# Two projections moved from the front into the attention, and the maxima taken 76 scores ahead instead of 80

## The chip, the cores and the metric

The kernel runs on one core of one Trainium2 chip. The metric is the device time of one execution in microseconds, the median of the runs shown. A profiled execution gives the engines' instructions: PE is TensorE (PEld its weight loads), DVE is VectorE, ACT is ScalarE, POOL is GpSimd, SP is SyncE, whose queue issues nearly all DMAs here. An engine takes its instructions in the order in which the program emits them, and so does each queue.

## The reference

One transformer block with adaptive norms, in float32, over 2048 rows of 512 columns:

```
mod = silu(c) @ w_mod                      # six vectors: sa, ca, ga, sb, cb, gb
h = layernorm(x) * (1 + ca) + sa
q, k, v = split(h @ wqkv)                  # 32 heads of 16 columns
o = softmax(q k^T / 4) v                   # full attention, 2048 x 2048 a head
x = x + ga * (o @ wo)
h = layernorm(x) * (1 + cb) + sb
x = x + gb * (gelu(h @ w1 + b1) @ w2 + b2) # 1792 hidden columns
```

## The kernel before, in words

The rows are cut into four blocks of 512 (NB, TB) and the 32 heads into eight groups of four. One block of queries against one group of heads is a unit, 32 in all (NU), in the order block 0 groups 0 to 7, block 1, and so on. Precision comes from splitting an operand into a high and a low part (tiles of two planes, "parts"); a projection of 128 output columns of one block of rows is then a group of twelve matmuls (terms3: four high-high, four low-high, four high-low).

**The front** is an order written out by hand (SCRIPT, lines 45 to 60). It norms and transposes the four blocks of rows, computes the modulation vectors, does the first projections (token G with kind, column group and block: G110 is the keys of column group 1 for block 0) and starts the maxima of the first unit's scores: token X emits two score matmuls (L390), token x one reduction on VectorE (L395). The front ends when LEAD score matmuls have been emitted.

**The attention** is 512 half-steps (half_step). The array is used as two halves of 64 rows. A half-step emits four score matmuls for the exponentials (L647, tile e, then exp on ScalarE, L654), four score matmuls for the maxima of a later unit (L390, tile mx, then a reduction on VectorE, L395), six matmuls of a background group if there is one (L276 through bg_mm), and last the value matmuls of the step before (pv, L681). A group of twelve full matmuls is 24 half matmuls, four half-steps. The maxima run LEAD scores ahead of what the half-steps alone would give: `nx = min(64 * NU, LEAD + 4 * (hs + 1))`. They use the PSUM banks 3, 4, 5 in turn (ring "mx"), the exponentials 0, 1, 2 (ring "e"), the background bank 7 (ring "bg").

When all 64 maxima of a unit are reduced, max_rows (lines 405 to 429) makes them into two rows beside the queries: a reduction (L407) and a 32x32 transposition (L409) on VectorE, then a copy and a subtraction on GpSimd (L411, L412) that split them in a high and a low part, then an SP store to memory (L416, three clock ticks later) and an SP load into the query tile (L422, six ticks later). The exponentials of the unit read these rows. A clock tick is one exponential; a half-step has four. Small waits are written as `later(n, f)`, n ticks.

Background work comes from a generator (work, lines 998 to 1014): block0 yields the projections left over from the front (the list plan), then comes front(b) (output projection, residual, layer norm and transposes of query block b) and feed(b) (its feed-forward part). A generator that yields None leaves a half-step without background work. block0 ends when all is stored, and open_ffn then closes the front's and the projections' pools and opens those of the feed-forward; output and feed-forward weights are fetched from then on (wload, one DMA a half-step at most). Transposes in front(0) are emitted as jobs of their own; for later blocks they go on the list `sides`, one at the end of a half-step. tick copies on VectorE (L1113) order the two halves of the array.

When the last score has been emitted (about 20 half-steps before the end) the half-steps carry four exponentials, four background matmuls and the value matmuls ("ending"). After the attention the rest of the background work of block 2 and all of block 3 follow on the full array.

The lines that the prediction's steps touch:

```
LEAD = 80                                                               # line 39
gp.tensor_copy(m2[:, 0], mt)                                            # line 411
gp.tensor_tensor(m2[:, 1], mt, m2[:, 0].bitcast(F32), op=ALU.subtract)  # line 412
(gp if b or t < 3 else ve).tensor_scalar(xn[t], ...)                    # line 830
plan = [(1, 1, [3]), (2, 1, [0, 1, 2, 3])]                              # line 971
plan += [(0, k, range(1, NB)) for k in range(KC)]                       # line 973
```

Of the kernel before, what the change touches and what calls it, by code (L numbers as in the profile page):

```python
# [8 lines left out]
F32 = mybir.dt.float32  # L9
FR = mybir.dt.float32r  # L10
AF = mybir.ActivationFunctionType
ALU = mybir.AluOpType
# [26 lines left out]
LEAD = 80  # L39
# [31 lines left out]
def block_kernel(ctx: ExitStack, tc: tile.TileContext, x, wqkv, wo, w1, b1, w2, b2, c, w_mod, out):  # L71
# [73 lines left out]
    pccm, pcpool = pool("pc", side="right")  # L145
    hcm, hpool = pool("hT", side="right")

# [28 lines left out]
    def load_x(b, q=sy):  # L176

        xin[b] = rows_tile(b, "lo", "xin", (P, 4, D), F32)
        for t in range(0, 4, 1 if b == 0 else 4):
            r0, n = b * TB + t * P, 1 if b == 0 else 4  # L180
            q.dma_start(xin[b][:, t : t + n], x[r0 : r0 + n * P, :].rearrange("(t p) d -> p t d", p=P))
# [223 lines left out]
    def max_rows(u):  # L405
# [5 lines left out]
        gp.tensor_copy(m2[:, 0], mt)  # L411
        gp.tensor_tensor(m2[:, 1], mt, m2[:, 0].bitcast(F32), op=ALU.subtract)  # L412
# [68 lines left out]
    def low_x(b, f, e):  # L481
        if hT[b][1] is None:
            hT[b][1] = rows_tile(b, "lo", "hTlo")
# [333 lines left out]
    def front(b, x2):  # L817
# [9 lines left out]

        def norm(t):
            xn[t] = tmp("xn")
            (gp if b or t < 3 else ve).tensor_scalar(  # L830
                xn[t], x2[t], mv[:, t, 0:1], rs[t], op0=ALU.subtract, op1=ALU.mult)
            later(40, lambda: gp.tensor_tensor(x2[t], x2[t], b2_b, op=ALU.add))
            if b and len(xn) == 4:
                later(9, lambda: sides.extend([lambda fc=fc: trans(fc, "mx") for fc in range(KC)]))

        def stat(t):
            if b == 0 and t == 3:
                ln_stat(mv, t, x2[t])
                later(1, lambda: factor(t))
                return  # L840
# [10 lines left out]
            later(4, lambda: part(1))  # L851
            later(8, whole)

        def factor(t):
# [3 lines left out]
            later(3 if t < 3 else 2, lambda: norm(t))  # L858

        for t in range(4):  # L860

            def evac(ps, t=t):
# [3 lines left out]
                def add():  # L866
                    gp.tensor_tensor(x2[t], y, x2[t], op=ALU.add)
                    later(8 if b or t < 3 else 3, lambda: stat(t))
# [5 lines left out]
        t0 = clock["t"]  # L874

        def trans(fc, bk="bg"):
# [11 lines left out]
        if b:  # L888
            yield from until(lambda: len(turned) == KC and clock["t"] >= turned[KC - 1] + 8)
            return  # L890
# [414 lines left out]
```

## Time and profile before

| what | value |
|---|---|
| median of three runs | 1687.38 us (1687.36 to 1691.88) |
| the profiled execution's own time | 1688.29 us |
| its span, first to last instruction | 1686.5 us |
| mean granted TensorE clock | 0.997 |
| PE busy | 1667.1 us, 99% |
| DVE busy | 1403.2 us, 83% |
| ACT busy | 1239.3 us, 73% |
| POOL busy | 691.9 us, 41% |
| first exponential matmul of the attention (L647) | at 101.36 us |
| first work after the attention | about 1564 us |

A row of the timeline gives start, length, engine, line, operation, tiles (out<-in), shapes and count; in brackets the engine's idle time just before and who ended it. A row of the groups ends in busy time in us, mean length of one in ns, and idle time before. A row of a stretch gives its length and then busy time and count of PE, PEld, DVE, ACT and POOL in it, the granted clock, the DMA share and GB/s.

### The profile page before, as it was taken

To read this page: it belongs to the slowest core of one execution; us is meant where nothing else is said; L and a number is where in the kernel's file an instruction comes from. 1 tells how busy PE (TensorE), PEld (TensorE's weight loads), DVE (VectorE), ACT (ScalarE), POOL (GpSimd) and SP (SyncE) were. 2 spreads that over 40 slices of the span, in tenths; PEclk is the share of its full clock that TensorE was granted. 3 is DMA by queue.
4 is the path that set the end of the run, shared out by engine and by line. 5 is a ranking of instruction groups with operands and counts; after the bars stand their busy time and mean duration, and the time that the engine had idled before them with its cause. 6 is when DMAs were issued, how large, how long until landed. Compare 5 with 4: busy or idle time off the path is not lost.

```text
span 1686.5 us, 32216 instructions
## 1 busy us (share of the span) xinstructions
PE 1667.1 (99%) x12103; PEld 917.0 (54%) x12103; DVE 1403.2 (83%) x2690; ACT 1239.3 (73%) x2381; POOL 691.9 (41%) x698
## 2 busy tenths in 40 slices
PE   7999999999999999999999999999999999999999
PEld 6655555555554455555555555555555555553777
DVE  7998888889899988898999888889999889891332
ACT  3367888778777788778877888778877788779131
POOL 7433534435121456415633456306633466226110
PEclk9999999999999999999999999999999999999999
DMA  8766766757457534426453464344363453343544
GB/s 293 200 213 184 223 195 201 235 172 221 146 160 214 121 99 109 103 57 156 125 157 90 121 165 121 84 133 134 99 179 82 120 145 100 82 120 97 209 154 156
DMA packets 137127, 251.88 MB, mean 149 GB/s; under 512 B 25854, under 2 KB 45324, under 8 KB 136972
## 3 DMA queue, kind: packets, MB, share of 16 engines
q1 hardware_dynamic: 135984, 248.53, 50.9%
q8 instruction: 96, 1.57, 0.4%
q10 hardware_dynamic: 988, 1.29, 0.3%
q14 instruction: 59, 0.48, 0.1%
HBM read 188.49 MB, written 61.28 MB: 148 GB/s over the span
## 4 chain that ended last, share of the span: by engine, by line
PE 94%; DVE 3%; DMA 1%; ACT 1%; issue 0%; SPq 0%; DVEq 0%; ACTq 0%
PE bg L276 40%; PE pv L681 30%; PE e L647 16%; PE mx L390 4%; PE pr L276 2%; DVE mxp L395 2%; ACT p L654 1%; PE o L276 1%; PE mx L335 0%; DMA wm<-in_w_mod_dram 0%; DVE hTlo L484 0%; DMA wo<-wos 0%; DVE bst L237 0%; DMA kh<-qk 0%; PE mx L879 0%
## 5 line engine op out<-in xcount | busy, mean ns | idle before, releaser
L395 DVE TENSOR_REDUCE mxp<-mx 128x1 f32<-128x512 f32 x2034 | 1286.2, 683 | 145.4 <-PE mx L390 130.1
L654 ACT ACTIVATE p<-e 128x512 f32<-128x512 f32 x2048 | 1073.0, 608 | 271.7 <-PE mx L390 250.5
L390 PE MATMUL mx<-kh,qst 48*128 48x512 f32 x2034 | 836.5, 422 | 0.8 <-DVE mxp L395 0.5
L647 PE MATMUL e<-qst,kh 50*128 50x512 f32 x2048 | 778.4, 424 | 3.1 <-ACT p L654 3.1
L647 PEld LDWEIGHTS e<-qst,kh 50*128 50x128 f32 x2048 | 341.4, 185 | 430.5 <-ACT p L654 310.2
L681 PE MATMUL pv<-p,vg 128*32 128x512 f32 x4096 | 546.3, 605 | 0.3 <-ACT osb L668 0.3
L390 PEld LDWEIGHTS mx<-kh,qst 48*128 48x128 f32 x2034 | 367.8, 185 | 14.9 <-DVE mxp L395 9.7
L276 PE MATMUL bg<-w,g 64*128 64x512 f32 (+1 forms) x1056 | 263.8, 388 | 0.0
L276 PEld LDWEIGHTS bg<-w,g 64*128 64x128 f32 (+1 forms) x1056 | 196.0, 186 | 29.3
L276 PE MATMUL bg<-pchi,w 64*128 64x512 f32 (+1 forms) x656 | 177.4, 390 | 0.0
L681 PEld LDWEIGHTS pv<-p,vg 128*32 128x32 f32 x4096 | 81.0, 108 | 172.7 <-issue 159.9
L276 PE MATMUL bg<-hThi,wqkv 64*128 64x512 f32 x560 | 153.2, 392 | 0.0
L276 PEld LDWEIGHTS bg<-pchi,w 64*128 64x128 f32 (+1 forms) x656 | 120.9, 185 | 23.6 <-DVE tick L1091 4.2
L276 PEld LDWEIGHTS bg<-hThi,wqkv 64*128 64x128 f32 x560 | 103.7, 185 | 12.5
L923 POOL TENSOR_SCALAR s<-s 128x512 f32<-128x512 f32 x40 | 59.9, 1497 | 90.3 <-ACT s L921 89.6
L942 POOL TENSOR_TENSOR x<-y,x 128x512 f32<-128x512 f32 x28 | 36.1, 1288 | 144.0 <-ACT y L941 143.8
L276 PE MATMUL bg<-pclo,w 64*128 64x512 f32 (+1 forms) x328 | 88.9, 389 | 0.0
L276 PE MATMUL bg<-hTlo,wqkv 64*128 64x512 f32 x280 | 76.6, 392 | 0.0
L276 PEld LDWEIGHTS bg<-pclo,w 64*128 64x128 f32 (+1 forms) x328 | 60.0, 184 | 13.6 <-DVE tick L1091 4.2
L916 POOL TENSOR_TENSOR s<-h 128x512 f32<-128x512 f32 x40 | 41.7, 1042 | 61.9 <-ACT h L915 61.9
L276 PE MATMUL bg<-wo,pchi 64*128 64x512 f32 x192 | 59.5, 389 | 0.6 <-DMA wo<-wos 0.6
L276 PEld LDWEIGHTS bg<-hTlo,wqkv 64*128 64x128 f32 x280 | 51.6, 184 | 7.5
(164 smaller groups left out, 1324.3 us busy)
## 6 DMA issues: line engine op xcount, KB each, us to landing
kh<-qk SPq DMA_DIRECT2D x256, 192.0 KB
w<-w1s SPq DMA_DIRECT2D x56, 512.0 KB
w<-w2s SPq DMA_DIRECT2D x54, 512.0 KB
vg<-v SPq DMA_DIRECT2D x64, 332.0 KB
qk<-parts SPq DMA_DIRECT2D x32, 512.0 KB
qst<-qk SPq DMA_DIRECT2D x64, 192.0 KB
qk<-parts SPq DMA_DIRECT2D x32, 256.0 KB
ou<-osb SPq DMA_DIRECT2D x32, 256.0 KB
```

The lines of the kernel that those rows point to most:

```text
L276: return te.matmul(ps, term[0][r], term[1][r], start=i == 0, stop=i == n - 1)
L390: te.matmul(ps, qst[u][r0 : r0 + KR, p, qc * P : (qc + 1) * P], kh(u, kr // 2)[r0 : r0 + KR, p, (kr % 2) * TB : (kr % 2 + 1) * TB], start= ...
L395: ins = ve.tensor_reduce(mxp[u][:, hc, kr : kr + 1], ps, axis=AX.X, op=ALU.max, negate=True)
L647: ins = te.matmul(ps, kh(u, kc // 8)[r0 : r0 + KX, p, (kc % 8) * P : (kc % 8 + 1) * P], qst[u][r0 : r0 + KX, p], start=True, stop=True)
L654: op = ac.activation(t, ps, AF.Exp, scale=SCALE)
L681: te.matmul(cur["ps"][32 * j : 32 * (j + 1)], vg[u][:, kc, j * VW : j * VW + 32], pt.pop(4 * s + j), start=kc == 0, stop=kc == NKC - 1)
L916: gp.tensor_tensor(s, h, h, op=ALU.mult)
L923: gp.tensor_scalar(s, s, 1.0, None, op0=ALU.add)
L942: later(4, lambda: gp.tensor_tensor(x2[t], y, x2[t], op=ALU.add))
```

## The change

Two groups of the front, the keys of column group 1 for blocks 1 and 2 (G111 and G112 with their evacuations and stores), leave the written order and go to the head of block0's plan. The maxima start 76 instead of 80 scores ahead, and the last tokens of the order lose two X and four x. The last four groups of the plan (queries of block 3, all four column groups) are taken out of it and kept as `deferred`; they are handed out wherever block0 or front(0) would have left a half-step without work (`filled`). For that the rows of block 3 and the projection weights move into a pool of eight pieces that stays open and is later used by the feed-forward's hidden tiles, and the pools are opened by try_open at the head of a half-step instead of at block0's end. A deferred group writes its result over its own weights.

In front(0) the fourth rows get their statistics in two parts like the others, with shorter distances (`short`), their norm runs on GpSimd instead of VectorE, and the transposes go over `sides` as for the later blocks. In max_rows the copy and the subtraction run on VectorE for every unit but the first.

```
-LEAD = 80
+LEAD = 76
...
-ml1 x G111 md1 x*4 A111.a X0*2 R111.a X0 G112 x D111.g x*2 O111 x*2 A112.a X0 x X0 R112.a pa2 x D112.g x pb2 x
-O112 x c2.a X1*2 x X1 mb0 x om x mb1 me0.a x U203 me1.a x*2 C203 X1*2 x X1 O203 G202 x*3 lm x*2
-Y202.a X1 x*2
+ml1 x md1 x*4 X0*2 x*3 X0 x*2
+X0 pa2 x*2 X0 pb2 x*3 c2.a X1*2 x X1 mb0 x om x mb1 me0.a x U203 me1.a x*2 C203 X1*2 G202 x O203 x lm x*2
+Y202.a
...
+    def piece_tile(name, i=None, dt=FR):
+        if i is None:
+            i = gn[0] % 8
+            gn[0] += 1
+        return ggpool.tile([P, 2, TB], dt, tag=f"g{i}", name=name, bufs=1)
...
-    hT = [[rows_tile(b, "hi", "hThi"), None] for b in range(NB)]
+    hT = [[rows_tile(b, "hi", "hThi"), None] for b in range(NB - 1)] + [[Rows("h3", 0), None]]
...
-    wslots = [wpool.tile([P, 2, KC, P], FR, name=f"wqkv{i}") for i in range(4)]
+    gslots = [piece_tile(f"wqkv{i}", 4 + i) for i in range(4)]
+    wslots = [t.rearrange("p a (k n) -> p a k n", n=P) for t in gslots]
...
-        gp.tensor_copy(m2[:, 0], mt)
-        gp.tensor_tensor(m2[:, 1], mt, m2[:, 0].bitcast(F32), op=ALU.subtract)
+        e = ve if u else gp
+        e.tensor_copy(m2[:, 0], mt)
+        e.tensor_tensor(m2[:, 1], mt, m2[:, 0].bitcast(F32), op=ALU.subtract)
...
+        def short(t):
+            return b == 0 and t == 3
+
         def norm(t):
             xn[t] = tmp("xn")
-            (gp if b or t < 3 else ve).tensor_scalar(
-                xn[t], x2[t], mv[:, t, 0:1], rs[t], op0=ALU.subtract, op1=ALU.mult)
+            gp.tensor_scalar(xn[t], x2[t], mv[:, t, 0:1], rs[t], op0=ALU.subtract, op1=ALU.mult)
...
-            if b and len(xn) == 4:
-                later(9, lambda: sides.extend([lambda fc=fc: trans(fc, "mx") for fc in range(KC)]))
+            if len(xn) == 4:
+                later(9 if b else 6, lambda: sides.extend([lambda fc=fc: trans(fc, "mx") for fc in range(KC)]))
...
-            later(4, lambda: part(1))
-            later(8, whole)
+            later(2 if short(t) else 4, lambda: part(1))
+            later(4 if short(t) else 8, whole)
...
-        if b:
-            yield from until(lambda: len(turned) == KC and clock["t"] >= turned[KC - 1] + 8)
-            return
-        yield from until(lambda: len(xn) == 4 and clock["t"] >= t0 + 9)
-        for fc in range(KC):
-            yield lambda fc=fc: trans(fc)
-        yield from wait(4)
+        yield from until(lambda: len(turned) == KC and clock["t"] >= turned[KC - 1] + (8 if b else 5))
...
-        plan = [(1, 1, [3]), (2, 1, [0, 1, 2, 3])]
+        plan = [(1, 1, [1, 2, 3]), (2, 1, [0, 1, 2, 3])]
...
-        plan += [(0, k, range(1, NB)) for k in range(KC)]
+        plan += [(0, k, range(1, NB - 1)) for k in range(KC)]
...
-        yield from until(lambda: not preps and not owed[0] and not vrows and not busy[0])
-        open_ffn()
+        deferred.extend((k, gslots[(len(plan) - KC + k) % 4]) for k in range(KC))
+        over0[0] = True
+        yield from until(lambda: "f" in pools)
...
+    def proj_late():
+        k, parts = deferred.pop(0)
+
+        def evac(ps):
+            r = tmp("pf") if "f" in pools else stage("pf")
+            ac.activation(r, ps, AF.Copy)
+            gp.tensor_copy(parts[:, 0], r)
+            gp.tensor_tensor(parts[:, 1], r, parts[:, 0].bitcast(F32), op=ALU.subtract)
+            later(8, lambda: store_qk(0, k, NB - 1, parts))
+
+        return proj_terms(0, k, NB - 1), "bg", evac
+
+    def filled(js):
+        for j in js:
+            yield proj_late() if j is None and deferred else j
+
+    def try_open():
+        if over0[0] and "f" not in pools and not preps and not owed[0] and not vrows and not busy[0]:
+            open_ffn()
...
-        yield from block0()
+        yield from filled(block0())
...
-            for j in fronts[b]:
+            for j in filled(fronts[b]):
...
+            while deferred:
+                yield proj_late()
...
+        try_open()
         if h or len(wt) < len(used) + KC:
             wload()
```

More of the change, by code (lines that the diff above doesn't have):

```diff
@@ L176, in load_x @@
     def load_x(b, q=sy):
-        xin[b] = rows_tile(b, "lo", "xin", (P, 4, D), F32)
-        for t in range(0, 4, 1 if b == 0 else 4):
-            r0, n = b * TB + t * P, 1 if b == 0 else 4
+        xin[b] = rows_tile(b, "lo", "xin", (P, 4, D), F32) if b < NB - 1 else Rows("x3", 2, F32)
+        n = 1 if b == 0 else 2 if b == NB - 1 else 4
+        for t in range(0, 4, n):
+            r0 = b * TB + t * P
             q.dma_start(xin[b][:, t : t + n], x[r0 : r0 + n * P, :].rearrange("(t p) d -> p t d", p=P))
@@ L857, in factor @@
             gp.tensor_tensor(rs[t], rs[t], mhalf[:, 0:1], op=ALU.pow)
-            later(3 if t < 3 else 2, lambda: norm(t))
+            later(2 if short(t) else 3, lambda: norm(t))
         for t in range(4):
@@ L873, in front, with trans @@
         drop(b, *[("o", k) for k in range(KC)])
-        t0 = clock["t"]
-        def trans(fc, bk="bg"):
+        def trans(fc, bk):
             ps = take(bk)
@@ L1279, in block_kernel @@
     assert not any(hooks.values())
-    close(tcm, pools["cm"], pccm, kqcm)
+    close(tcm, pools["cm"], ggcm, pccm, kqcm)
 _INS = ["A_x", "A_wqkv", "A_wo", "B_w1", "B_b1", "B_w2", "B_b2", "c", "w_mod"]
```

25 lines of the change are left out of this document (17 added, 8 removed).

## The prediction

> **What bounds the kernel now.** I read the page first (busy time, then the chain of waits), then the timeline half-step by half-step, then the groups of VectorE and GpSimd.
>
> ```profile
> PE 1667.1 (99%) x12103; PEld 917.0 (54%) x12103; DVE 1403.2 (83%) x2690; ACT 1239.3 (73%) x2381; POOL 691.9 (41%) x698
> PE 94%; DVE 3%; DMA 1%; ACT 1%; issue 0%; SPq 0%; DVEq 0%; ACTq 0%
> ```
>
> TensorE is 94% of the chain that ended last: what holds back one of its matmuls is paid in full, and what another engine does behind it is free. The attention consists of 512 half-steps, each closed by one value block (pv, L681), so the distance between two starts of L681 is the length of a half-step. In the timeline, first two of the six waiting half-steps without background work, then the one after a unit's 64 maxima are complete (L407, L409):
>
> ```profile
> 516.66 1.07 PE L681 MATMUL pv<-p,vg 128*32 128x512 f32 x8
> 519.27 1.06 PE L681 MATMUL pv<-p,vg 128*32 128x512 f32 x8
> ...
> 600.92 1.06 PE L681 MATMUL pv<-p,vg 128*32 128x512 f32 x8
> ...
> 602.24 0.22 DVE L407 TENSOR_REDUCE mn<-mxp 128x16 f32<-128x64 f32 x1
> 602.49 0.21 DVE L409 STREAM_TRANSPOSE mt<-mn 128x32 f32<-128x32 f32 x1
> 602.63 1.84 DVE L395 TENSOR_REDUCE mxp<-mx 128x1 f32<-128x512 f32 x3
> ...
> 603.76 1.06 PE L681 MATMUL pv<-p,vg 128*32 128x512 f32 x8
> ```
>
> A half-step with six background matmuls takes 603.76 - 600.92 = 2.84 us, one without takes 519.27 - 516.66 = 2.61. In the full one the first reduction after L409 starts 602.63 - 600.92 = 1.71 us after pv and costs nothing. The same place one unit earlier, where a bn_stats of 0.39 us happens to stand between L409 and that reduction:
>
> ```profile
> 553.89 1.07 PE L681 MATMUL pv<-p,vg 128*32 128x512 f32 x8
> ...
> 555.45 0.21 DVE L409 STREAM_TRANSPOSE mt<-mn 128x32 f32<-128x32 f32 x1
> 555.59 0.39 DVE L844 BATCH_NORM_STATS2 bsh<-x 128x6 f32<-128x256 f32 x1
> 555.89 1.87 DVE L395 TENSOR_REDUCE mxp<-mx 128x1 f32<-128x512 f32 x3
> ...
> 556.62 0.18 PEld L390 LDWEIGHTS mx<-kh,qst 48*128 48x128 f32 x1 [0.28 <-DVE mxp L395]
> 557.05 1.06 PE L681 MATMUL pv<-p,vg 128*32 128x512 f32 x8
> ```
>
> The reduction starts 2.00 us after pv, 0.29 later than above; the fourth score matmul, which needs the bank of the first (three banks in the ring "mx"), waits for it; the half-step takes 557.05 - 553.89 = 3.16 us, 0.32 more. So at this place the slack of VectorE is used up: **each us put between L409 and the next reduction costs a us of the kernel**. The change puts two instructions there.
>
> **The change part by part.**
>
> *1. The pair at L411 and L412 moves from GpSimd to VectorE for units 1 to 31.* On GpSimd it is off the path. On VectorE it stands in front of the reduction just discussed, thirty times (unit 31's is followed by no score).
>
> ```profile
> L729 DVE RECIPROCAL dn<-dn 128x32 f32<-128x32 f32 x16 | 5.5, 344 | 0.0
> L409 DVE STREAM_TRANSPOSE mt<-mn 128x32 f32<-128x32 f32 x32 | 6.8, 212 | 2.9 <-POOL pclo L749 0.5
> L1113 DVE COPY tick<-mx 128x1 f32<-128x1 f32 x362 | 53.6, 148 | 0.0
> ```
>
> Before has neither instruction on VectorE. Bounds: 0.15 us each (the copy of one column, L1113) to 0.34 (the reciprocal of the same 128x32); I take 0.20, just under the transpose of the same size. Each reads what the one before wrote, and such a step costs the duration and 0.03 more (602.24 + 0.22 = 602.46, L409 starts 602.49). A pair is then 2 x 0.23 = 0.46 us (0.36 to 0.74); thirty are 13.8 us (10.8 to 22.2). Below nothing is excluded: nothing is taken off VectorE.
>
> To this comes GpSimd's hold on VectorE. Small VectorE instructions in the front, and what GpSimd ran:
>
> ```profile
> 21.62 1.59 POOL L208 TENSOR_TENSOR wqkv<-wraw,wqkv 128x512 fp32r<-128x512 f32 x1
> ...
> 22.69 0.55 DVE L451 TENSOR_SCALAR rs<-mv 128x4 f32<-128x4 f32 x1
> ...
> 47.37 0.16 DVE L451 TENSOR_SCALAR rs<-mv 128x4 f32<-128x4 f32 x1
> ```
>
> L451 takes 0.16 us with GpSimd idle, but 0.55 where GpSimd is in L208, and ends at 23.24, within 0.03 of GpSimd's end at 23.21. I looked at the thirty places where the pair will stand (0.25 us after each L409, one half-step later, since LEAD falls by one half-step's four scores); the first of them and the sum:
>
> ```profile
> 141.30:141.80 0.50, 0.50 (x8) 0.43 (x6) 0.50 (x2) 0.50 (x2) 0.38 (x1) 1.00 0.05 16
> ...
> sum 15.10, PE 14.69 PEld 13.06 DVE 15.10 ACT 15.10 POOL 6.37; mean PE 0.49 PEld 0.44 DVE 0.50 ACT 0.50 POOL 0.21
> ```
>
> GpSimd (fifth) is busy in 6.37 of 15.10 us, with work other than the pair itself at the start of 13 of the thirty. What runs there is mostly of this kind:
>
> ```profile
> L924 POOL TENSOR_TENSOR h<-s,h 128x512 f32<-128x512 f32 x40 | 51.3, 1283 | 3.3
> ```
>
> Half of 1.28 us is left to run on average: 13 x 0.64 = 8.3 us. If the next GpSimd instruction slips in between copy and subtraction it is about as much again; if small instructions slip past GpSimd, nothing. I take 8.3, because the nearest row, L451, waited to the end.
>
> [...]
>
> What waits behind the pair: three reductions, the tick (L1113) and the fourth score, hence pv. SP's store of the maxima (L416) no longer waits for GpSimd's queue.
>
> *2. LEAD 80 to 76 and two projections out of the front.* Four reductions and two groups of twelve matmuls go.
>
> ```profile
> 87.11 3.68 DVE L395 TENSOR_REDUCE mxp<-mx 128x1 f32<-128x512 f32 x6 [0.72 <-PE mx L390]
> 91.00 2.48 DVE L395 TENSOR_REDUCE mxp<-mx 128x1 f32<-128x512 f32 x4 [0.21 <-PE mx L390]
> ...
> 93.91 7.22 DVE L395 TENSOR_REDUCE mxp<-mx 128x1 f32<-128x512 f32 x12
> ...
> 97.61 0.56 SPq L422 DMA_DIRECT2D qst<-m  x2
> ...
> 101.36 0.40 PE L647 MATMUL e<-qst,kh 50*128 50x512 f32 x1
> ...
> 101.56 1.97 DVE L395 TENSOR_REDUCE mxp<-mx 128x1 f32<-128x512 f32 x3 [0.42 <-PE mx L390]
> ```
>
> The two groups hold TensorE 6 us, but VectorE is busy there but for 0.72 + 0.21 + 0.42 us, so only these gaps and four reductions of 7.22 / 12 = 0.60 can be won: 3.8 us at most. The first exponential also needs unit 0's maxima back from memory (L422 issued 97.61, 3.8 us ahead of it), and that chain moves by the first two gaps alone; about 1 us of its 3.8 is spare. I take -2.3 (-0.9 to -3.8).
>
> *3. Two more projections in the attention, the last four after block 0.* A group is four half-steps of six. By the plan in block0 and the starts of L681: before, 35 groups fill half-steps 0 to 139, six wait, output projections run 146 to 161, eight wait or only transpose, and the feed-forward starts at 170. After, 33 groups fill 0 to 131 and three deferred ones 132 to 143; the pools open at 138 (the last division, 9 half-steps after unit 7, sets it), output runs 144 to 159, the fourth deferred one 160 to 163, transposes 164 to 167, and the feed-forward again starts at 170: its wait is counted in clock ticks from the last output group. So **both projections go into half-steps that waited**, and the work left for the end stays the same. Eight half-steps turn full: 8 x (2.84 - 2.61) = +1.8 us. Their evacuations (ScalarE, two GpSimd instructions, two SP stores each) lie beside matmuls; SP's other loads have half-steps to spare.
>
> *4. The stalls of this stretch.*
>
> ```profile
> 576.68 1.07 PE L681 MATMUL pv<-p,vg 128*32 128x512 f32 x8
> 580.49 1.06 PE L681 MATMUL pv<-p,vg 128*32 128x512 f32 x8
> 583.89 1.06 PE L681 MATMUL pv<-p,vg 128*32 128x512 f32 x8
> 586.81 1.07 PE L681 MATMUL pv<-p,vg 128*32 128x512 f32 x8
> ```
>
> and in the chain of waits between the first two of them:
>
> ```profile
> 577.46 1.35 DVE xn L830
> ```
>
> The norm of the fourth rows on VectorE (L830) and its whole bn_stats make two half-steps 3.81 and 3.40 where 2.61 and (with a block of transposes, the third distance) 2.92 are usual: 1.7 us, gone when GpSimd norms and the statistics come in halves. The transposes now come from the side list, out of the ring of the scores; between 0 and 0.4 us each, four of them: +0.4. Output projections start six instead of four half-steps after their weights are asked for, which may save a wait there. Together -1.7 (-2.5 to 0).
>
> *5. The end of the scores* comes one half-step later.
>
> ```profile
> 1520.70 1.07 PE L681 MATMUL pv<-p,vg 128*32 128x512 f32 x8
> 1522.83 1.06 PE L681 MATMUL pv<-p,vg 128*32 128x512 f32 x8
> ```
>
> One of 2.84 us stands for one of 2.13 without scores, +0.7, and its two more background matmuls shorten a later one: +0.5.
>
> Sum: 13.8 + 8.3 - 2.3 + 1.8 - 1.7 + 0.5 = **+20.4 us**. The profiled execution took 1688.29 us (span 1686.5 and 1.8 around it), the median of the runs 1687.38; I put the sum on the median: about 1707.5.
>
> **The rivals.**
>
> *The lock does not bite* (20%): the pair slips past GpSimd as L1113 always does. 20.4 - 8.3 = +12.1: 1699.5.
>
> *The pair is absorbed, not slower* (12%). Place: the wait of the fourth score for the first reduction. L407 and L409 already stand there and cost nothing at 1.71 us after pv. If the pair overlaps its neighbours, the rest decides: -2.3 + 1.8 - 1.7 + 0.5 = -1.7, 1685.7. It decides below 1.7 / 30 = 0.06 us a unit. Against it: the 0.28 us at 556.62.
>
> *The maxima come late* (6%): with 76 scores ahead a unit's maxima are complete one half-step later, and the key load due at step 14 goes into SP's queue ahead of L422.
>
> ```profile
> 605.61 0.55 SPq L422 DMA_DIRECT2D qst<-m  x2
> ...
> 613.27 0.50 PE L647 MATMUL e<-qst,kh 50*128 50x512 f32 x1
> ```
>
> L422 is issued 7.7 us ahead of its exponential; 2.84 less leaves 4.8. Each 0.5 us by which it then lands late costs 30 x 0.5 = 15 on top: 1722.5.
>
> *The deferral does not do what it says* (7%): a late opening pushes the feed-forward past 170, and a displaced group of twelve matmuls returns at the end, where it costs 12 x 0.23:
>
> ```profile
> 1604.69 78.22 PE bg L276 x336
> ```
>
> Two groups: +5.6, 1713.
>
> **How the numbers follow.** Forecast 55%: 1707.5, and its own range with the bounds of the pair and the lock is 1697 to 1719. A measurement of this kernel tells about 0.3%, 5 us, from no change. Slower by more needs above 1692.4: forecast, lock-free case, late maxima and deferral nearly whole, 81%. Within: the absorbed case and a little of the lock-free one, 14%. Faster, where the absorbed case meets the front's best: 5%. The range reaches down to 1689 for a cheap pair without lock, and up to 1719.
>
> **What would show it.** Right: half-steps after L409 of 3.3 us, near 4 where GpSimd is busy, PEld L390 waiting there for DVE mxp; copies on VectorE of 0.2 us, or up to 1 beside GpSimd; the feed-forward starting at half-step 170; no L830 on VectorE. Wrong: these half-steps staying at 2.84, or the first exponential of the units waiting for L422, or a first exponential of the attention earlier than 97.5.

## The result and the profile after

The changed kernel takes 1726.87 us (median of 4 runs, 1724.97 to 1729.14) against 1688.81 (median of 4 runs, 1687.36 to 1691.88) for the kernel before: a ratio of 1.0224, 95% interval 1.0211 to 1.0236. Forecast were 1707.5 and a range up to 1719; the direction was right, the size half of what it is. The profiled execution took 1728.32 us, its span is 1726.5, 40.0 more than the span before.

From the page of the changed kernel, the busy times, the chain by engine, and the group of the exponentials' score matmuls (L672; before it was L647, and its idle time of 3.1 us had no DMA in it):

```profile
PE 1686.4 (98%) x12127; PEld 924.5 (54%) x12127; DVE 1417.2 (82%) x2757; ACT 1241.4 (72%) x2379; POOL 681.3 (39%) x639
...
PE 88%; DVE 6%; DMA 4%; SPq 1%; issue 1%; ACT 0%; DVEq 0%; ACTq 0%
...
L672 PE MATMUL e<-qst,kh 50*128 50x512 f32 x2048 | 786.8, 426 | 16.5 <-DMA qst<-m 14.2
```

TensorE fell from 94% to 88% of the chain; VectorE doubled to 6%, and transfers rose from 1% to 4%. The last column says where: 14.2 us of L672's idle time ended with qst<-m, the load of the maxima rows.

To place the 40 us I took the starts of the 512 value blocks in both traces and subtracted the lengths of the half-steps, as in the prediction. Half-step n here is the one that ends with value block n, counted from 0; the prediction's numbers are one higher. The columns are: the front (start of value block 0); the half-steps just behind a unit's maxima (n mod 16 = 11, 12, 13); those at the first exponential of a unit (31, 32, 47, 79, 80, 143, 144, 399); those at unit 6's new keys (83, 84, 87, 88); 102 to 107, where one wait falls in e6 and e8 below (107 stands under the pair in the other rows); the last 22; and all else. The column of the rows holds the late keys too where these fall on 79 and 80, as in e3. All are differences to before, in us of the profiled execution.

| kernel | median, ratio | front | pair | rows | keys | 102-107 | end | else | sum |
|---|---|---|---|---|---|---|---|---|---|
| changed | 1726.9, 1.0224 | -0.9 | +15.0 | +14.8 | +3.7 | 0 | +6.2 | +1.2 | +40.0 |
| e1 pair on GpSimd | 1714.8, 1.0161 | -2.0 | +1.2 | +17.5 | +0.9 | 0 | +6.4 | +0.6 | +24.7 |
| e2 lead 80 | 1716.9, 1.0174 | -1.2 | +23.5 | +0.5 | +3.0 | 0 | 0 | +1.0 | +27.0 |
| e3 lead 80, pair on GpSimd | 1696.7, 1.0049 | +0.8 | +0.6 | +3.9 | +1.6 | 0 | 0 | +1.1 | +8.0 |
| e4 before + pair on VectorE | 1714.6, 1.0157 | +0.9 | +23.5 | 0 | 0 | 0 | 0 | +0.7 | +25.1 |
| e5 before + lead 76 | 1705.1, 1.0098 | -1.5 | +0.7 | +10.1 | 0 | 0 | +7.5 | -1.3 | +15.5 |
| e6 e3, both groups in front | 1695.0, 1.0037 | -0.5 | +0.3 | +0.8 | 0 | +6.0 | 0 | -1.6 | +5.0 |
| e7 changed, rows early | 1713.4, 1.0146 | -2.4 | +15.7 | +1.0 | +1.0 | 0 | +6.8 | +0.9 | +23.0 |
| e8 e3, one group in front | 1701.8, 1.0080 | -0.5 | +1.0 | +4.6 | 0 | +8.2 | 0 | -0.9 | +12.3 |
| e9 e5, rows early | 1697.7, 1.0045 | -1.8 | +0.7 | +0.1 | 0 | 0 | +8.4 | +1.4 | +8.7 |
| e10 e7, pair on GpSimd | 1698.5, 1.0047 | +0.4 | +1.2 | +0.7 | +4.6 | 0 | +7.7 | +1.9 | +16.5 |
| e11 before + norm | 1688.7, 0.9994 | +0.9 | +0.9 | 0 | 0 | 0 | -0.1 | -1.4 | +0.2 |
| e12 e4, pair split | 1707.4, 1.0102 | -0.3 | +18.7 | +0.1 | 0 | 0 | 0 | +0.9 | +19.3 |

Two things, then, cost about 15 us each, and the second, which was a rival of 6% in the prediction, also costs 6.2 at the end. Each ratio is to runs of the kernel before beside it (medians 1688.28 to 1690.08); the 95% intervals are within 0.0018 of the ratios. The profiled execution of e10 took 1704.8 us, its other three 1697.8 to 1698.8; its row holds some 6 us that the median does not.

**The pair.** The timeline of the changed kernel around unit 11's maxima, answering to the two places shown in the prediction:

```profile
672.88 1.06 PE L706 MATMUL pv<-p,vg 128*32 128x512 f32 x8
...
675.73 1.06 PE L706 MATMUL pv<-p,vg 128*32 128x512 f32 x8
...
676.02 0.21 DVE L433 STREAM_TRANSPOSE mt<-mn 128x32 f32<-128x32 f32 x1
676.27 0.18 DVE L436 CAST m<-mt 128x32 fp32r<-128x32 f32 x1
...
676.48 0.19 DVE L437 TENSOR_TENSOR m<-mt,m 128x32 fp32r<-128x32 f32 x1
...
677.93 0.18 PEld L414 LDWEIGHTS mx<-kh,qst 48*128 48x128 f32 x1 [0.22 <-DVE mxp L419]
...
678.96 1.06 PE L706 MATMUL pv<-p,vg 128*32 128x512 f32 x8
```

The half-step with the pair takes 678.96 - 675.73 = 3.23 us, the one before it 675.73 - 672.88 = 2.85; PEld L414, the load of the fourth score, waits for VectorE. As forecast, copy and subtraction take 0.18 and 0.19 and start 0.25 and 0.46 after L433. Their groups (busy us, mean ns, idle before them), in which a few long ones raise the means to 231 and 223 ns:

```profile
L436 DVE CAST m<-mt 128x32 fp32r<-128x32 f32 x31 | 7.2, 231 | 1.1
...
L437 DVE TENSOR_TENSOR m<-mt,m 128x32 fp32r<-128x32 f32 x31 | 6.9, 223 | 1.1
```

**The rows.** The same view at unit 5, the costliest place. L322 and L323 store a projection's query or key rows, L386 loads keys, L441 stores and L447 loads the maxima rows; all these stand in SP's one queue:

```profile
332.95 0.47 SPq L323 DMA_DIRECT2D qk<-parts  x1
...
333.33 0.21 DVE L433 STREAM_TRANSPOSE mt<-mn 128x32 f32<-128x32 f32 x1
...
337.41 0.79 SPq L386 DMA_DIRECT2D kh<-qk  x2
...
338.72 1.37 SPq L441 DMA_DIRECT2D m<-m  x2
...
339.17 1.07 PE L706 MATMUL pv<-p,vg 128*32 128x512 f32 x8
...
342.84 0.54 SPq L447 DMA_DIRECT2D qst<-m  x2
...
344.60 0.76 PE L672 MATMUL e<-qst,kh 50*128 50x512 f32 x1 [4.37 <-DMA qst<-m]
...
347.89 1.93 PE L706 MATMUL pv<-p,vg 128*32 128x512 f32 x8
```

and, of what SP's queue waited for between 332 and 345 us (us in total, times, longest):

```profile
SPq L386 <- DMA qk<-parts: 3.9, 1, 3.9
```

Copy and subtraction follow L433 at once, so the rows are ready before 334.1. But the key load L386, next in SP's queue, waits 3.9 us for what L322 and L323 have just stored to land, and is issued at 337.41. The rows are stored at 338.72 only, come back by L447 at 342.84, and the first exponential waits for them until 344.60. The half-step takes 347.89 - 339.17 = 8.72 us, 3.50 before. At unit 2 SP stands still behind a value load, at unit 9 weights, keys, rows of x and the store of a deferred projection stand ahead. Part of each delay is the landing of the rows' own store, for which SP waits before L447: 2.4 us at unit 5, 2.8 at unit 2, 4.6 at unit 9.

**The end.** The last unit has only short half-steps ahead (2.6 and 2.1 us, since scores run out one half-step before):

```profile
1556.22 1.29 POOL L942 TENSOR_TENSOR g<-h,g 128x512 fp32r<-128x512 f32 x1
1556.25 1.29 DVE L436 CAST m<-mt 128x32 fp32r<-128x32 f32 x1
...
1557.57 1.17 SPq L441 DMA_DIRECT2D m<-m  x2
...
1560.23 0.57 SPq L447 DMA_DIRECT2D qst<-m  x2
...
1562.19 0.47 PE L672 MATMUL e<-qst,kh 50*128 50x512 f32 x1 [3.02 <-DMA qst<-m]
```

Here the copy waited for GpSimd's L942, to within 0.03 us of its end, and the first exponential waited 3.02 us for the rows.

**The front.** It gave 0.9 of the 2.3 us. Windows of the changed kernel (busy us of TensorE, its weight loads, VectorE, ScalarE, GpSimd; then the granted clock, DMA share and GB/s), and the timeline within them:

```profile
84.50:88.00 3.50, 2.60 (x7) 0.91 (x5) 3.50 (x8) 0.00 (x0) 0.00 (x0) 1.00 1.04 397
88.00:91.40 3.40, 3.34 (x12) 0.77 (x11) 3.40 (x7) 0.00 (x0) 0.00 (x0) 0.50 0.19 71
91.40:94.80 3.40, 3.40 (x16) 1.03 (x14) 2.56 (x6) 0.60 (x1) 0.46 (x2) 0.50 0.00 0
```

```profile
85.29 3.78 PE L414 MATMUL mx<-kh,qst 48*128 48x512 f32 x6 [0.49 <-DVE mxp L419]
...
89.00 1.93 PE L256 MATMUL pr<-wm,s_m 128*32 128x512 f32 x8
...
91.59 1.93 PE L256 MATMUL pr<-wm,s_m 128*32 128x512 f32 x8
```

Without the two groups TensorE has only six score matmuls to do between 85.3 and 89 and waits for VectorE's banks between them; from 88.0 to 94.8 its granted clock is 0.50, where the same windows of before show 1.00. The two groups of eight of L256 behind it take 1.93 us each; before, sixteen took 1.92 together.

### The profile page after: what moved, and what is told of

The parts are those of the page before. It is cut to its first block, busy times and chain, and to the rows that moved or that the text cites. A ratio compares the mean times of both kernels' runs of the same rounds, so it can differ in the third digit from the quotient of the medians.

```text
span 1726.5 us, 32229 instructions
## 1 busy us (share of the span) xinstructions
PE 1686.4 (98%) x12127; PEld 924.5 (54%) x12127; DVE 1417.2 (82%) x2757; ACT 1241.4 (72%) x2379; POOL 681.3 (39%) x639
## 4 chain that ended last, share of the span: by engine, by line
PE 88%; DVE 6%; DMA 4%; SPq 1%; issue 1%; ACT 0%; DVEq 0%; ACTq 0%
PE bg L300 38%; PE pv L706 27%; PE e L672 15%; PE mx L414 4%; DVE mxp L419 4%; DMA m<-m 1%; PE pr L300 1%; DMA qk<-parts 1%; DMA qst<-m 1%; PE o L300 1%; PE mx L359 0%; DMA wm<-in_w_mod_dram 0%; DMA kh<-qk 0%; PE pr L256 0%; PE mx L901 0%
## 5 line engine op out<-in xcount | busy, mean ns | idle before, releaser
L414 PE MATMUL mx<-kh,qst 48*128 48x512 f32 x2038 | 847.3, 426 | 4.1 <-DVE mxp L419 2.0
L672 PE MATMUL e<-qst,kh 50*128 50x512 f32 x2048 | 786.8, 426 | 16.5 <-DMA qst<-m 14.2
L672 PEld LDWEIGHTS e<-qst,kh 50*128 50x128 f32 x2048 | 344.5, 186 | 445.2 <-ACT p L679 310.3
L414 PEld LDWEIGHTS mx<-kh,qst 48*128 48x128 f32 x2038 | 371.7, 186 | 24.0 <-DVE mxp L419 16.4
L300 PE MATMUL bg<-hThi,wqkv 64*128 64x512 f32 x432 | 117.9, 391 | 1.4 <-DVE tick L1156 1.2
L300 PEld LDWEIGHTS bg<-hThi,wqkv 64*128 64x128 f32 x432 | 79.4, 185 | 13.2 <-DVE tick L1156 3.0
L300 PEld LDWEIGHTS bg<-pclo,w 64*128 64x128 f32 (+1 forms) x328 | 60.3, 185 | 13.5 <-DVE tick L1134 3.4
L300 PE MATMUL bg<-hTlo,wqkv 64*128 64x512 f32 x216 | 58.0, 388 | 0.0
L1156 DVE COPY tick<-mx 128x1 f32<-128x1 f32 x368 | 54.5, 148 | 0.3 <-PE mx L414 0.3
```

The lines of the kernel that those rows point to most:

```text
L300: return te.matmul(ps, term[0][r], term[1][r], start=i == 0, stop=i == n - 1)
L414: te.matmul(ps, qst[u][r0 : r0 + KR, p, qc * P : (qc + 1) * P], kh(u, kr // 2)[r0 : r0 + KR, p, (kr % 2) * TB : (kr % 2 + 1) * TB], start= ...
L672: ins = te.matmul(ps, kh(u, kc // 8)[r0 : r0 + KX, p, (kc % 8) * P : (kc % 8 + 1) * P], qst[u][r0 : r0 + KX, p], start=True, stop=True)
L1156: saw(ve.tensor_copy(tick, mxb[0][:, :1]))
```

## The experiments

**Taking the two suspects out, one by one and together.** e1 puts the pair back on GpSimd:

```diff
-        e = ve if u else gp
+        e = gp
```

> The changed kernel with copy and subtraction of the maxima (L436, L437) back on GpSimd for every unit; 76 scores ahead and the moved projections stay. Two theories share the 38 us that the change cost (1688.8 to 1726.9): the pair on VectorE lengthens the half-step after each unit's maxima (sum of those half-steps +19.6 us, about 0.45 a pair by itself = 13.5), and the maxima rows come late for the first exponential (the long half-steps 31, 79, 80, 143, 493, 494 sum to +19). By the first theory alone (the pair is the cause, the rows are late because of it too) nearly all comes back: about 1695. By both together only the pair comes back and the rows are as late as before or later, since GpSimd may start the pair up to 1.3 us later than VectorE did: 1713 to 1722, with the long half-steps still there. If the lock were the main price, 1727 - 8 - 14 = 1705.

Measured: 1714.79, 12.1 less than the changed kernel. The column of the pair goes from +15.0 to +1.2, that of the rows stays (+17.5). So the rows are not late because of the pair, and "nearly all comes back" is out.

e2 goes back to 80 scores ahead, the pair stays on VectorE:

```diff
-LEAD = 76
+LEAD = 80
-... C203 X1*2 G202 x O203 x lm x*2 Y202.a
+... C203 X1*2 x X1 O203 G202 x*3 lm x*2 Y202.a X1 x*2
```

> The changed kernel with 80 scores ahead, as it was (LEAD 80 and the end of the front's order as it was); the pair stays on VectorE, the two projections stay in the attention. Theory: the rows come late because with 76 ahead the time between the load of the rows and their first exponential fell from 7.4 to 3.4 us; 4 us more margin takes away the long half-steps at units 2, 9 and 31 (2.7 + 5 + 4.9) and most of unit 5's 6.5, and costs 1 to 2.4 us in the front: 1727 - 17 + 2 = about 1712. The late keys of unit 6 (half-steps 87, 88, +3.5) stay. Rival: the moved projections fill SP's queue at these places whatever the lead; then the long half-steps stay, and it is 1724 to 1728.

Measured: 1716.88, 10.0 less. The rows come in time (+0.5) and the end is as before (0.0), 20 us won where the theory had 17; but the pair now costs 23.5 instead of 15.0, which neither theory had. The step from 80 to 76 had moved the pair out of the way of something.

e3 has both edits.

```diff
-LEAD = 76
+LEAD = 80
...
-        e = ve if u else gp
+        e = gp
```

> Both put back (80 scores ahead, pair on GpSimd): left of the change are the two projections in the attention, the four deferred ones and the norm. If pair and late rows add: 1727 - 17 + 2 - 14 = about 1698 to 1700, that is still 10 slower than before, of which 3.5 are the late keys at half-steps 87 and 88. If the moved projections are worth what I had put on them (front -2.3, half-steps +1.8, stalls -1.7), about 1687 to 1690. If they are the cause of the late rows, above 1705.

Measured: 1696.69, ratio 1.0049 (1.0032 to 1.0066). Of the 38 us 30 are gone; 8 stay with the moved projections. Some 5.5 of them (columns of the rows and the keys) are the keys of unit 6, projected eight half-steps later than before (half-steps 79, 80, 83). In e3's timeline:

```profile
331.19 0.45 SPq L323 DMA_DIRECT2D qk<-parts  x1
...
335.43 1.06 PE L706 MATMUL pv<-p,vg 128*32 128x512 f32 x8
...
335.72 0.81 SPq L386 DMA_DIRECT2D kh<-qk  x2
...
339.77 0.47 PE L414 MATMUL mx<-kh,qst 48*128 48x512 f32 x1 [2.85 <-DMA kh<-qk]
...
342.09 1.93 PE L706 MATMUL pv<-p,vg 128*32 128x512 f32 x8
```

The key load L386 is issued 4.1 us behind the store L323 that it reads, and the score matmul L414 waits 2.85 us for it. The half-step takes 342.09 - 335.43 = 6.66 us.

**The pair alone.** e4 is the kernel before with the pair on VectorE:

```diff
-        gp.tensor_copy(m2[:, 0], mt)
-        gp.tensor_tensor(m2[:, 1], mt, m2[:, 0].bitcast(F32), op=ALU.subtract)
+        e = ve if u else gp
+        e.tensor_copy(m2[:, 0], mt)
+        e.tensor_tensor(m2[:, 1], mt, m2[:, 0].bitcast(F32), op=ALU.subtract)
```

> The kernel before with one edit: copy and subtraction on VectorE for units 1 to 31. The price of the pair alone. By 0.45 us for each of 30 pairs: +13.5, 1702; if GpSimd's hold on VectorE is the main thing at these places: +20 or more, 1709; if the pair is absorbed where the rows are not late: 1689. No long half-step at the first exponential of a unit, since the rows still have 7 us.

Measured: 1714.56, 26.3 more than before: above the 13.5 of the bare pair, as only the theory of GpSimd's hold had it. Its groups, and the timeline of e4 at unit 4:

```profile
L412 DVE CAST m<-mt 128x32 fp32r<-128x32 f32 x31 | 14.0, 450 | 1.1
...
L413 DVE TENSOR_TENSOR m<-mt,m 128x32 fp32r<-128x32 f32 x31 | 8.8, 283 | 1.1
```

```profile
284.02 1.07 PE L682 MATMUL pv<-p,vg 128*32 128x512 f32 x8
...
285.53 1.29 POOL L312 TENSOR_TENSOR parts<-pf,parts 128x512 fp32r<-128x512 f32 x1
...
285.77 1.10 DVE L412 CAST m<-mt 128x32 fp32r<-128x32 f32 x1
...
286.79 1.26 POOL L614 TENSOR_TENSOR wf<-wf,gb_b 128x512 f32<-128x512 f32 x1
...
286.90 1.20 DVE L413 TENSOR_TENSOR m<-mt,m 128x32 fp32r<-128x32 f32 x1
288.02 1.87 DVE L395 TENSOR_REDUCE mxp<-mx 128x1 f32<-128x512 f32 x3
...
289.18 1.07 PE L682 MATMUL pv<-p,vg 128*32 128x512 f32 x8
```

The copy takes 1.10 us and ends at 286.87, GpSimd's L312 at 286.82; the subtraction takes 1.20 and ends at 288.10, GpSimd's L614 at 288.05. The half-step takes 289.18 - 284.02 = 5.16 us. Over the 62 instructions the time above 0.185 us each sums to 11.2 us, against 2.6 in the changed kernel. So the hold that the prediction priced at 8.3 us, and calls the lock in a rival, is real and dear: both the cast and the two-input subtraction wait here, until 0.05 us after GpSimd's end. In the changed kernel it mostly does not meet anything (four of the 62 instructions take more than 0.21 us there): with 76 ahead the pair comes 4 us nearer to its unit's first exponential, past the subtraction L312 of the projections, which with 80 ahead starts just ahead of the copy at five of the twelve copies that are held.

**The lead alone.** e5 is the kernel before with 76 scores ahead and the front's order that goes with it:

```diff
-LEAD = 80
+LEAD = 76
-... C203 X1*2 x X1 O203 G202 x*3 lm x*2 Y202.a X1 x*2
+... C203 X1*2 G202 x O203 x lm x*2 Y202.a
```

> The kernel before with one edit: 76 scores ahead instead of 80 (with the front's order that goes with it); the projections stay in the front, the pair on GpSimd. With the projections in the attention the same step from 80 to 76 cost 18 us (1696.7 against 1714.8, both with the pair on GpSimd): front about -2.8, late rows +21 (half-steps 31, 47, 79, 80, 143, 399, 493, 494). Theory A: the lead alone makes the rows late, whatever stands in SP's queue: +15 to +18, 1704 to 1706. Theory B: the rows are late only where SP's queue is held by a transfer that the moved projections brought there (units 2, 5, 9), and the lead alone leaves the places without projections (399, 493, 494: +6): 1688 - 2.8 + 6 = 1691, up to 1697 if one other half-step collides.

Measured: 1705.14; theory A's figure, not B's. Rows are late at 31, 79 and 399 (+10.1) and at the end (+7.5) with the projections still in the front. The lead makes the rows late; the moved projections only add places (143, and more at 79).

**Is it the place in SP's queue?** e7 is the changed kernel with the rows' store and load put into SP's queue earlier:

```diff
-            later(3, store)
-            later(6, load)
+            later(1, store)
+            later(2, load)
```

> The changed kernel with the store of the maxima issued 1 instead of 3 exponentials after the pair and their load 2 instead of 6: both come earlier in SP's queue (load 4 exponentials, about 2.8 us), nothing else changes. If the place in SP's queue and the margin make the rows late, the long half-steps 31, 143, 493 lose 2 to 2.8 us each and 79 up to that: 1727 - 7 to - 11 = 1716 to 1720. If the store's wait (for the pair) or the DMA's landing sets it and not the queue, nothing changes, 1727; if the load, which waits on SP for the store to land, holds up key loads behind it, up to 1735.

Measured: 1713.38, 13.5 less, more than the forecast 7 to 11. The rows column falls from +14.8 to +1.0; the end stays at +6.8. The answer to unit 5 above, in e7's timeline:

```profile
328.71 0.47 SPq L323 DMA_DIRECT2D qk<-parts  x1
...
329.53 1.42 SPq L441 DMA_DIRECT2D m<-m  x2
...
333.94 0.57 SPq L447 DMA_DIRECT2D qst<-m  x2
...
334.61 0.79 SPq L386 DMA_DIRECT2D kh<-qk  x2
...
338.67 0.47 PE L414 MATMUL mx<-kh,qst 48*128 48x512 f32 x1 [1.36 <-DMA kh<-qk]
...
339.54 1.07 PE L706 MATMUL pv<-p,vg 128*32 128x512 f32 x8
```

L441 now goes ahead of the key load, and no exponential waits; what is left of that half-step (4.63 us) is the late keys (L414). So for the middle of the kernel the order in the queue was it: in the median unit the second load stands as far ahead of the first exponential as without the edit (3.44 us against 3.39). Where the rows were late, they also land sooner once they go ahead: from store to load 3.10 us instead of 4.45 at unit 2, 2.68 instead of 6.69 at unit 9. The waiting on SP and the transfers already under way are not told apart by this run. At the end the order was not it: there the chain of copy, subtraction, store, landing, load and landing is longer than the half-steps left (with the same early rows in e9 below, 4.80 us from the copy at 1524.36 to the exponential at 1529.16, where a half-step takes 2.60).

e9 does the same to e5:

```diff
-LEAD = 80
+LEAD = 76
...
-            later(3, store)
-            later(6, load)
+            later(1, store)
+            later(2, load)
```

> The kernel before with 76 scores ahead (1705.1 by itself) and the store of the maxima rows issued 1 exponential after the pair instead of 3, their load 2 instead of 6. Theory: with the lead alone the loss (+16) is rows that reach memory and come back too late at five places (half-steps 31, 79, 399, 493, 494: +15) and nothing else, and the front is 1.5 shorter; 4 exponentials (2.8 us) earlier in SP's queue take away the 3.0, 2.7 and 1.3 us of waiting at 31, 79 and 399 and most at 493: 1689 to 1692. If the earlier load only blocks SP until the store has landed and pushes other loads back, 1700 or more.

Measured: 1697.68. The rows column falls from +10.1 to +0.1, the end keeps +8.4, which I had expected to fall too, so the time lies between the two forecasts; against before it is still 1.0045 (1.0030 to 1.0060). e10 is e7 with the pair on GpSimd:

```diff
-        e = ve if u else gp
+        e = gp
...
-            later(3, store)
-            later(6, load)
+            later(1, store)
+            later(2, load)
```

> The changed kernel with the pair on GpSimd and the rows stored and loaded earlier (1 and 2 exponentials after the pair). Beside the run with the pair on VectorE and the same early rows (1713.4) it prices the pair where no rows are late: 30 x 0.45 and about 3 of waiting for GpSimd, 1713.4 - 16 = 1697. If the rows come late again because GpSimd starts the pair later than VectorE, 1700 to 1705. Late keys of unit 6 (half-steps 79, 83, 87) stay in both.

Measured: 1698.52, 14.9 below e7 (forecast 16): the price of the pair with 76 ahead where rows are not late; the late keys of unit 6 stay in both.

**Is there slack beside the pair?** e12 is e4 with the subtraction one half-step behind the copy:

```diff
-        e.tensor_tensor(m2[:, 1], mt, m2[:, 0].bitcast(F32), op=ALU.subtract)
+        def low():
+            e.tensor_tensor(m2[:, 1], mt, m2[:, 0].bitcast(F32), op=ALU.subtract)
+        later(4 if u else 0, low)
...
-            later(3, store)
-            later(6, load)
+            later(6, store)
+            later(9, load)
```

> The kernel before with the pair on VectorE (1714.6 by itself), but the subtraction four exponentials (one half-step) after the copy, store and load of the rows three exponentials later. Two parts of the 26 us are to be told apart. By the theory of no slack at this place (0.2 us of slack a half-step, the pair takes 0.45) each of the two instructions fits by itself, and what is left is the wait for GpSimd's instruction at about nine copies (0.9 each) and half-steps of other stalls: 1698 to 1704. If it is the wait for GpSimd that costs nearly all, and now hits copy and subtraction apart, it stays at 1712 to 1718.

Measured: 1707.36, between the two answers, so neither holds. A copy that meets nothing still lengthens its half-step by 0.22 us (half-steps 171, 187, 331: 3.06 to 3.07 instead of 2.84), its own length and no less: there is no slack for even one of the two at this place. One half-step later there is: a subtraction that meets nothing there costs nothing (half-steps 172, 220, 268: 2.84). But sixteen of the 31 subtractions meet instructions of GpSimd at their new place, and the time above 0.185 us of the 62 instructions sums to 19.1 us, against 11.2 in e4.

**The moved work.** e6 is e3 with both projections back in the front, so only the four deferred ones and the new norm are left:

```diff
-        plan = [(1, 1, [1, 2, 3]), (2, 1, [0, 1, 2, 3])]
+        plan = [(1, 1, [3]), (2, 1, [0, 1, 2, 3])]
```

> Of the change only the four deferred query projections with the new tiles and GpSimd's norm with halved statistics are left: 80 scores ahead, pair on GpSimd, both projections in the front as before. By my terms (two half-steps of 3.81 and 3.40 back to usual, four transposes in the scores' ring +0.3 each, four to eight half-steps from 2.61 to 2.84): between -2 and +1, 1686 to 1689, no long half-step at 79, 80, 83. If the deferral itself cost part of the 8.4 us of the run with lead and pair put back, it stays above 1692.

Measured: 1695.01, a miss: 1.0037 (1.0022 to 1.0052) where no difference was expected. The keys are in time again, but one wait is new, in e6's timeline:

```profile
398.51 0.43 SPq L212 DMA_DIRECT2D wraw<-in_A_wqkv_dram  x1
...
402.38 1.07 PE L706 MATMUL pv<-p,vg 128*32 128x512 f32 x8
...
407.36 1.06 ACT L216 ACTIVATE wqkv<-wraw 128x512 fp32r<-128x512 f32 x1 [4.22 <-DMA wraw<-in_A_wqkv_dram]
...
408.95 0.50 PE L672 MATMUL e<-qst,kh 50*128 50x512 f32 x1 [3.94 <-ACT p L679]
...
409.61 1.93 PE L706 MATMUL pv<-p,vg 128*32 128x512 f32 x8
```

L212 fetches the next projection weight, now earlier than before, since only two groups are left for each of these weights; it is issued at 398.51, takes until 407.3 to land, and the cast L216 of ScalarE stands 4.22 us waiting for it, with the exponentials behind it in ScalarE's queue. The half-step takes 409.61 - 402.38 = 7.23 us. The cast's turn comes 4.6 us behind the issue of its load (at 403.1); in before the shortest such distance in the attention is 7.9 us, and nothing waits. So the deferral's order leaves this weight too little time, and e11, which has not got it, has no such wait. e11 is the kernel before with nothing but the new `front`:

```diff
-            (gp if b or t < 3 else ve).tensor_scalar(
-                xn[t], x2[t], mv[:, t, 0:1], rs[t], op0=ALU.subtract, op1=ALU.mult)
+            gp.tensor_scalar(xn[t], x2[t], mv[:, t, 0:1], rs[t], op0=ALU.subtract, op1=ALU.mult)
...
-            if b == 0 and t == 3:
-                ln_stat(mv, t, x2[t])
...
-        for fc in range(KC):
-            yield lambda fc=fc: trans(fc)
```

> The kernel before with nothing but the new division of the first block's norm (GpSimd for all rows, statistics of the last rows in halves, transposes from the side list). The run with these and the four deferred projections was 5.7 slower than before, with one wait of ScalarE for a weight (half-steps 102, 103: +5.9). By my reading that wait belongs to the deferral's order of the weight loads, and the norm itself takes away the 3.68, 3.81 and 3.40 half-steps at 147, 163, 164: -1 to -2, 1686 to 1688. If the norm costs, 1690 or more.

Measured: 1688.71 against 1690.08, ratio 0.9994 (0.9985 to 1.0003): half-step 163 loses what was forecast (3.80 to 2.62), 164 only falls from 3.40 to 3.20, and 165 to 167, with the transposes in the scores' ring, rise from 2.92 to 3.2. The whole gain is 1 to 2 us and not told apart from nothing. None of the other edits gave so fast a kernel, and it is no faster than before by this measurement.

e8 is e3 with one of the two groups (G111) back in the front:

```diff
-ml1 x md1 x*4 X0*2 x*3 X0 x*2 X0 pa2 x*2 X0 pb2 x*3 c2.a
+ml1 x G111 md1 x*4 A111.a X0*2 R111.a X0 x D111.g x*2 O111 x X0 x pa2 x*2 X0 pb2 x*3 c2.a
...
-        plan = [(1, 1, [1, 2, 3]), (2, 1, [0, 1, 2, 3])]
+        plan = [(1, 1, [2, 3]), (2, 1, [0, 1, 2, 3])]
```

> 80 scores ahead, pair on GpSimd, and one of the two moved projections back in the front: the keys of unit 6 are projected four half-steps earlier than in the run with both in the attention (1696.7), four later than before. Theory: those 8.4 us are the late keys of unit 6 (half-steps 79, 80, 83, 87, together +7 over their usual length, key loads that wait for stores issued 5 us ahead); four half-steps are 11.4 us, more than the 3 us by which they were late, so they vanish: 1688 to 1690. Rival: the slow clock and waits in the front take it (first value block at 107.6 against 106.8): then 1694 or more.

Measured: 1701.80, another miss, though its theory of the keys was right (column of the keys 0.0, half-step 79 at 2.85). ScalarE waits 5.93 us for a weight at half-step 106, as in e6 (its turn comes 1.7 us behind the issue), and unit 9's rows are late at 143 (6.58 us) even with 80 ahead. With both groups in the attention (e3) neither of the two happens. Shifting the groups by four half-steps each time brought another pair of transfers together; what each shift costs, 5 to 12 us here, was not to be read from the half-steps that it fills.

## Why the prediction was right and wrong

1. *The pair*: right. Copy and subtraction at 0.20 each were 0.18 and 0.19, the half-step 3.23 instead of about 3.3, the fourth score waits for VectorE. The column of the pair, less what e1 keeps of it, is 15.0 - 1.2 = 13.8 us with 1.5 us of the hold in it (units 1 to 30), so the bare pair was about 12.3 where 13.8 were forecast.
2. *GpSimd's hold* (8.3 us): the wait was right (in e4 until 0.05 us after GpSimd's end), the size wrong, and the failed step was to look at the thirty places "0.25 us after each L409, one half-step later" in the trace of before, as if the pair came there and GpSimd's work stayed where it was. In the windows of half a microsecond from the start of each copy in the changed kernel (first of thirty, and their sum):

```profile
140.67:141.17 0.50, 0.50 (x10) 0.05 (x2) 0.46 (x3) 0.21 (x1) 0.00 (x0) 1.00 1.00 332
...
sum 15.00, PE 14.78 PEld 1.96 DVE 13.93 ACT 10.24 POOL 2.32; mean PE 0.49 PEld 0.07 DVE 0.46 ACT 0.34 POOL 0.08
```

GpSimd is busy 2.32 of 15.00 us there, not 6.37 of 15.10, and the waiting sums to 2.6 us, 1.1 of it at the copy of unit 31. The place explains a part: the pair stands 4.4 us nearer to the first exponential in e5 and 4.0 in the changed kernel (see 6), not one half-step of 2.84, and in windows of before taken 4.4 us later GpSimd is busy 4.93 of 15.00. The rest is that GpSimd's work moved too. Nor was the rival "the lock does not bite" right: with 80 ahead it costs 11.2 (e4).
3. *The front* (-2.3): -0.9, the small end of what was given. The first value block starts at 104.5 to 107.6 us in the six kernels of this study without the two groups, at 106.3 to 107.7 in the five with the front of before, so it is about 1 us and within the scatter. The two kernels with the lead alone changed start 1.5 and 1.8 us earlier than before (e5, e9), the two with the groups alone out 1.2 earlier and 0.8 later (e2, e3): what was won is the lead's as far as it shows, and a gain from the two groups is not shown. What the prediction had not seen is TensorE's clock, 0.50 from 88.0 to 94.8 us; what it costs in the front no run here tells apart.
4. *Deferral and stalls* (+1.8 and -1.7): right in the changed kernel as to the place, and a little too good. The feed-forward starts at the same half-step, 163 and 164 fall from 3.80 and 3.40 to 3.26 and 3.19, 147 from 3.68 to 2.84; but 165 and 166 rise from 2.92 to 3.2, so the stalls gave about -1.3 (147 and 163 to 167). What failed is the sentence that "SP's other loads have half-steps to spare": the keys of unit 6 had not (+3.7), and with other shifts a weight had not (e6, e8).
5. *The end* (+0.5): +6.2. That step failed too: it looked at TensorE's scores and not at the rows, whose chain does not get shorter when the half-steps do (5.94 us in the changed kernel, from the copy at 1556.25 to the exponential at 1562.19).
6. *The maxima come late* (6%): this happened, for +14.8 us, and is the main error, since the sum of the forecast put the rows at nothing. The place was named, the key load ahead of the rows in SP's queue. Two steps of the reckoning failed. The first is its size, "2.84 less leaves 4.8": the maxima do not come "one half-step later". In e5, where the lead alone changed, L409 stands 6.4 us ahead of its unit's first exponential in the median unit, in before 10.8. That is 4.4 us less, since L409 moves from 1.56 us behind a value block to 0.37 behind the second one after it; the second load of the rows then stands 2.9 us ahead instead of 7.3 (in the changed kernel 3.4). The second is the reckoning with one usual unit and one price for all thirty. Most units are in time; units 2, 5, 9 and 31 lose 2.7 to 6.5 us each. The trace of before had it to see: from the starts of L422 and of the first exponentials, the second load stands 7.3 us ahead in the median unit, but 4.5 at unit 7 and little more than 3 at unit 31. The worst units had to be taken, not the usual one.

Signs stated as wrong, "the first exponential of the units waiting for L422", came true together with those stated as right: forecast and rival added up, and the sum of the two, 1722.5, is what the rival had been given. That its 15 us are close to the measured 14.8 is luck: they were thirty units late by 0.5 us each, and it was a few units late by far more.

## What to carry to other kernels

A distance between a transfer and its user that is ample in a usual round (7.3 us in the median unit of before) says little about the worst one (little more than 3 at unit 31): look for the rounds in which a load in the same queue waits for a store issued just ahead of it, as L386 does for 3.9 us at unit 5, and count what stands behind. A shift counted in steps of the program is to be measured in time: one step of four scores moved the maxima by 4.4 us, about one and a half half-steps. Where work is moved by a few rounds, the trace of before no longer says what two engines do at the same moment; a price for their meeting, 2.6 us in the changed kernel and 11.2 in e4, needs both bounds in the range. Taking work out of a front that another engine bounds can come with a lower TensorE clock (0.50 from 88.0 to 94.8 us in the changed kernel and from 88.3 to 91.7 in e3, 1.00 there in before), and need not make the front shorter (0.9 us shorter in the changed kernel, 0.8 longer in e3).

## What the runs showed of the hardware

In the changed kernel TensorE's granted clock was 0.50 for 6.8 us from 344.0 us, and for 3.4 us each from 374.7, 542.0 and 1562.6, beginning in, or within 0.7 us of the end of, single waits of TensorE (4.37, 1.58, 3.31 and 3.02 us) in a loop that is otherwise full; it stayed at 1.00 at the wait of 2.63 us that ends at 198.66. In the front it was 0.50 from 88.0 to 94.8 us, behind a window in which TensorE was busy 2.60 of 3.50 us with seven matmuls. In e3 it was 0.50 from 88.3 to 91.7 us, behind a window of 2.50 busy us in 3.40, also with seven matmuls; in before, with the two groups in the front, it was 1.00 from 81 to 98 us. The busy time alone does not decide: from 197.2 to 200.6 us of the changed kernel TensorE was busy 1.95 of 3.40 us, with eighteen matmuls, and the clock stayed at 1.00. What does decide is not shown. At unit 5, where the clock fell, the late row cost more than its wait of 4.37 us: the eight value matmuls behind it took 1.93 us instead of 1.07. In e9 they took 1.93 us in two half-steps behind the wait of 3.12 us that ends at 1529.16.
